# Moving GpSimd's arithmetic to VectorE in a retention layer followed by two feed-forward layers

## The chip, the cores and the metric

The kernel runs on one core of a Trainium2 chip. The metric is the device time of one execution in microseconds, as the median of several runs. The engines are TensorE (PE in the profile; its weight loads are PEld), VectorE (DVE), ScalarE (ACT), GpSimd (POOL) and SyncE (SP), which issues most DMAs.

## What is computed

The input is q, k and v of a linear attention with decay (retention), of 2 batches, 8 heads, 768 positions and head size 64, and the weights of two feed-forward layers in float64.

```python
for t in range(S):
    state = gamma * state + einsum('bhd,bhe->bhde', k[:, :, t], v[:, :, t])
    y[:, :, t] = scale * einsum('bhd,bhde->bhe', q[:, :, t], state)
x = y.transpose(0, 2, 1, 3).reshape(1536, 512)
h = x @ w_in;   x = softplus(h) @ w_out              # first layer, 512 -> 2048 -> 512
h = x @ w2_in;  y = (h * clip(h + 3, 0, 6) / 6) @ w2_out   # second layer, the same sizes
```

## The kernel before

**Attention.** The 768 positions of each batch are cut into 6 chunks of 128; a batch and a chunk make a unit, 12 in all (u = 0 to 11). A unit transposes k and q on TensorE (`transposed`, line 194), multiplies q with k and masks the result on VectorE into the tile pt (`scores`, 208), multiplies the state of the chunks before, the tile bd, with q (`carry`, 220), lets the state fade by gamma (`fade`, 261), multiplies pt with the scaled v, the tile vs (`intra`, 230; vs is made in `decayed`, 202), and adds this chunk's k times vs to the state (`state`, 244). The result is scaled into the tile on (240) and split into two tiles that TensorE takes at its fast float32 form: x_hi, a rounded copy made by ScalarE (241), and x_lo, what the copy lost (242).

**Feed-forward layers.** The 1536 rows are three chunks of 512 columns, and the 2048 inner features are 16 groups of 128. A step is one group of one chunk: `gemm1` (332) does 12 products of 128x512 (w_hi with x_hi and x_lo, w_lo with x_hi, four times), ScalarE and VectorE make the activation g in 128x512 pieces (tiles g and e) and its parts hi and lo; `gemm2` (359) does 12 more products, for the group of two steps before. The first layer has 48 steps, the second 48.

**Weights.** They arrive as pairs of 32-bit words. `convert` (83) turns one 128x512 piece of them (tile raw) into float32: ScalarE scales the high words, VectorE clamps them (a TENSOR_SCALAR raw<-raw), shifts them (a TENSOR_SCALAR w<-raw), and two SCALAR_TENSOR_TENSOR w<-raw,w put sign and low bits in. Then w is split into w_parts: ScalarE writes the high part. For the first 8 pieces (`done[1] < 2 * EARLY`, 95) GpSimd subtracts it to get the low part (97); for the 56 others ScalarE writes minus the high part and GpSimd issues a DMA that adds w to it in memory (100). There are 64 pieces; 32 of them belong to the first layer.

**Order.** Units 0 to 3 run in program order (`InOrder` with `nc.on`). From unit 4 on, each unit is followed by one step of the first layer, the pieces of weights are fed by a fixed count (`first`, 141: 6 pieces after step 0 and two more after each further step), and the order on each engine is set by the framework's scheduler. An engine works through its list in order: an instruction that waits holds all behind it. Every helper call is recorded at line 31, so the profile has to be read by tiles.

Of the kernel before, what the change touches and what calls it, by code (L numbers as in the profile page):

```python
# [10 lines left out]
F32 = mybir.dt.float32  # L11
# [3 lines left out]
ALU = mybir.AluOpType  # L15
# [26 lines left out]
def kernel(ctx, tc, q, k, v, w1_in, w1_out, w2_in, w2_out, tq, tk, tc_, tg, out):  # L42
    nc = InOrder(tc)
    B, H, S, D = q.shape
    NT, DM = out.shape
    DFF = w1_in.shape[1]
    NP = H // 2
# [35 lines left out]
    def convert(m, o, f):  # L83

        raw = raws.pop((m, o, f))
        low, y = raw[:, :, 0], raw[:, :, 1]

        w = cv_p.tile([P, CH], U32, tag="w", name="w")
        nc.scalar.activation(y.bitcast(F32), y.bitcast(F32), AF.Copy, scale=2.0 ** -112)
        nc.vector.tensor_scalar(y.bitcast(F32), y.bitcast(F32), -TOP, TOP, ALU.max, ALU.min)  # L90
        nc.vector.tensor_scalar(w, y, 3, None, ALU.logical_shift_left)
        nc.vector.scalar_tensor_tensor(w, y, 0x80000000, w, ALU.bitwise_and, ALU.bitwise_or)
        nc.vector.scalar_tensor_tensor(w, low, 29, w, ALU.logical_shift_right, ALU.bitwise_or)
        t = (wout_p if o else win_p).tile([P, 2, CH], F32R, tag="w", name="w_parts")
        if done[1] < 2 * EARLY:
            nc.scalar.activation(t[:, 0], w.bitcast(F32), AF.Copy)
            nc.gpsimd.tensor_tensor(t[:, 1], w.bitcast(F32), t[:, 0].bitcast(F32), ALU.subtract)
        else:
            nc.scalar.activation(t[:, 1], w.bitcast(F32), AF.Copy, scale=-1.0)
            nc.gpsimd.dma_start(out=t[:, 1].bitcast(F32), in_=w.bitcast(F32), accum_op=ALU.add)  # L100
            nc.scalar.activation(t[:, 0], w.bitcast(F32), AF.Copy)
        if o:
            w_out_t[m, f] = t
        else:
            w_in_t[m, f] = t.rearrange("p a (k n) -> p a k n", k=KD)
# [13 lines left out]
    def feed(n):  # L119

        n = min(n, len(order))
        while done[1] < n:
            fetch_weights(done[1] + (1 if nc.on else 2))
            convert(*order[done[1]])
            done[1] += 1
# [19 lines left out]
    s = 0  # L145
# [11 lines left out]
def attention(ctx, tc, nc, q, k, v, tq, tk, tcc, tg, x_hi, x_lo, CH, bank, feed, fetch_weights):  # L157
    B, H, S, D = q.shape
    NP = H // 2
# [18 lines left out]
    tc_sb = const.tile([P, NP], F32, name="tc_sb")  # L178
# [22 lines left out]

    def decayed(u):
        vs = wk.tile([P, H, D], F32, tag="vs" + "0" * (u < START), name="vs", bufs=2)
        (nc.vector if u < 2 else nc.gpsimd).tensor_tensor(
            vs, nat["v", u], tk_sb.rearrange("p (h o) -> p h o", o=1).to_broadcast([P, H, D]), ALU.mult)
        tr["vs", u] = vs

# [12 lines left out]
    def carry(u):  # L220
        b, i = units[u]
        qT = tr["q", u]
        o = ps(NP, C)
        tr["o", u] = o
        if i > 0:
            for p in range(NP):
                nc.tensor.matmul(o[:, p, :], bd[b][:, p, :], qT[:, p, :], start=(p == 0), stop=False, skip_group_check=True)
        fade(u)

    def intra(u):  # L230
        b, i = units[u]
        vs, pt, o = tr["vs", u], tr["pt", u], tr["o", u]
        for h in range(H):
            g = h % 2
            nc.tensor.matmul(o[g * D:(g + 1) * D, h // 2, :], vs[:, h, :], pt[:, g, h // 2, :],
                             start=(i == 0 and h < 2), stop=True, skip_group_check=True)
        c, at = divmod(u * C, CH)
        hi, lo = x_hi[c][:, :, at:at + C], x_lo[c][:, :, at:at + C]
        on = wk.tile([P, NP, C], F32, tag="on" + "0" * (u < START), name="on", bufs=2)
        nc.vector.tensor_tensor(on, o, tq_sb, ALU.mult)  # L240
        nc.scalar.activation(hi, on, AF.Copy)
        nc.gpsimd.tensor_tensor(lo, on, hi.bitcast(F32), ALU.subtract)

    def state(u):
        b, i = units[u]
# [15 lines left out]
    def fade(u):  # L261
        b, i = units[u]
        if i == 0 or i == NCH - 1:
            return
        for j in range(2):
            r = slice(j * D, (j + 1) * D)
            s = bd[b][r, :, r]
            nc.gpsimd.tensor_tensor(s, s, tc_sb[r].rearrange("p (n o) -> p n o", o=1).to_broadcast([D, NP, D]), ALU.mult)

    for t in bd:  # L270
        nc.vector.memset(t, 0.0)
# [15 lines left out]
    def prepare(u):  # L287
        transposed(u, "k")
        transposed(u, "q")
        decayed(u)  # L290
# [9 lines left out]
    for u in range(START):  # L300
        scores(u)
        prepare(u + 1)
        carry(u)
        intra(u)
        state(u)
# [5 lines left out]
    def unit(u):  # L311
        scores(u)
        if u + 3 < len(units):
            fetch(u + 3, "k", "q", "v")
        if u + 1 < len(units):
            prepare(u + 1)
        carry(u)
        intra(u)
        state(u)
# [133 lines left out]
```

## Time and profile before

| | |
|---|---|
| median of 3 runs | 620.3 us (618.93, 620.3, 621.04) |
| the profiled execution's own time | 619.72 us |
| its span on the core | 617.9 us |
| TensorE busy | 595.0 us (96%) |
| VectorE busy | 353.6 us (57%) |
| ScalarE busy | 277.5 us (45%) |
| GpSimd busy | 102.2 us (17%), 48.9 us of it in issuing 56 DMAs |
| bytes moved by DMA | 61.60 MB |

The shares are means over stages that differ: the attention units take up the first 125 us, the conversion of the first layer's weights goes on to about 170 us, and the second layer's weights are converted between about 280 and 400 us. TensorE's columns in a stretch count a product from start to its modelled end, so neighbouring products overlap.

### The profile page before, as it was taken

Reading aid. Unit: us, or ns where it says so; the run is one execution under the profiler, and the core shown is the slowest. Engines: PE = TensorE matmul, PEld = TensorE weight load, DVE = VectorE, ACT = ScalarE, POOL = GpSimd, SP = SyncE. Lnnn points to the kernel's source line nnn. Section 1 sums busy time; section 2 is a strip of 40 time slices with the busy share of each in tenths; the row PEclk is TensorE's granted clock in tenths of the full one; section 3 lists DMA queues with packets and bytes.
Section 4 is the critical chain, followed back from the end, with each engine's and each line's share of the span. In section 5 each row is a group of like instructions: output and inputs, shape, how many; then the busy total and the mean of one; then the engine's idle time right before and its main releaser. Section 6 shows DMA issues by size and latency. Waiting matters only on the chain.

```text
span 617.9 us, 7766 instructions
## 1 busy us (share of the span) xinstructions
PE 595.0 (96%) x2963; PEld 489.4 (79%) x2963; DVE 353.6 (57%) x583; ACT 277.5 (45%) x473; POOL 102.2 (17%) x110
## 2 busy tenths in 40 slices
PE   7988787999999999999999999999999999999997
PEld 6866576788888888888877878888888888888886
DVE  4599999899863433366667799822422222322223
ACT  3354556578653333465556678722222222222220
POOL 1755455432100000011111123200000000000000
PEclk9999899999999999999999999999999999999999
DMA  9998877788810000045567789700100000100001
GB/s 194 232 235 229 207 183 188 175 216 209 198 37 1 0 1 1 0 95 128 136 152 188 162 203 256 148 0 1 53 16 0 2 1 0 69 0 1 0 1 68
DMA packets 69511, 61.60 MB, mean 100 GB/s; under 512 B 40033, under 2 KB 56673, under 8 KB 69473
## 3 DMA queue, kind: packets, MB, share of 16 engines
q1 hardware_dynamic: 61408, 46.42, 26.8%
q0 software_dynamic: 8064, 14.68, 14.4%
q8 instruction: 23, 0.38, 0.3%
q14 instruction: 16, 0.12, 0.1%
HBM read 43.26 MB, written 3.15 MB: 75 GB/s over the span
## 4 chain that ended last, share of the span: by engine, by line
PE 73%; DVE 14%; DMA 5%; issue 4%; ACT 3%; SPq 1%; POOL 0%; DVEq 0%; POOLq 0%; ACTq 0%
PE banks L31 73%; DVE w L31 6%; DMA raw<-in_moe_w_in_dram 3%; DVE raw L31 2%; DVE g L31 1%; DVE pt L31 1%; DVE e L31 1%; DMA q<-in_q_dram 1%; DVE lo L31 1%; DMA w_parts<-w 1%; ACT raw L31 1%; DVE bd L31 1%; ACT e L31 1%; ACT hi L31 1%; SPq L31 1%
## 5 line engine op out<-in xcount | busy, mean ns | idle before, releaser
L31 PE MATMUL banks<-x_hi,w_parts 128*128 128x512 f32 x768 | 254.6, 392 | 0.0
L31 PEld LDWEIGHTS banks<-x_hi,w_parts 128*128 128x128 f32 x768 | 144.7, 189 | 30.9 <-issue 0.7
L31 PE MATMUL banks<-x_lo,w_parts 128*128 128x512 f32 x384 | 150.2, 391 | 0.0
L31 PE MATMUL banks<-hi,w_parts 128*128 128x512 f32 x384 | 126.9, 391 | 5.3 <-ACT w_parts L31 3.0
L31 PE MATMUL banks<-w_parts,hi 128*128 128x512 f32 (+1 forms) x386 | 118.4, 388 | 0.5 <-DVE g L31 0.5
L31 DVE SCALAR_TENSOR_TENSOR g<-e,banks 128x512 f32<-128x512 f32 x48 | 33.0, 688 | 125.2 <-ACT e L31 125.2
L31 DVE TENSOR_TENSOR lo<-g,hi 128x512 fp32r<-128x512 f32 x96 | 67.3, 701 | 48.0 <-ACT hi L31 47.9
L31 DVE SCALAR_TENSOR_TENSOR w<-raw,w 128x512 uint32<-128x512 uint32 x128 | 92.4, 723 | 1.5
L31 POOL DMA_DIRECT2D w_parts<-w x56 | 48.9, 874 | 254.3 <-ACT w_parts L31 101.0
L31 ACT ACTIVATE e<-banks,three 128x512 f32<-128x512 f32 x48 | 32.9, 685 | 127.6 <-PE banks L31 127.6
L31 PEld LDWEIGHTS banks<-hi,w_parts 128*128 128x128 f32 x384 | 71.9, 188 | 21.5 <-ACT w_parts L31 3.3
L31 ACT ACTIVATE hi<-g 128x512 fp32r<-128x512 f32 x96 | 60.5, 631 | 56.5 <-DVE g L31 56.1
L31 ACT ACTIVATE w_parts<-w 128x512 fp32r<-128x512 f32 x120 | 70.2, 624 | 34.7 <-DVE w L31 34.2
L31 PEld LDWEIGHTS banks<-w_parts,hi 128*128 128x128 f32 x386 | 72.3, 188 | 15.9 <-DVE g L31 0.9
L31 PEld LDWEIGHTS banks<-x_lo,w_parts 128*128 128x128 f32 x384 | 72.4, 189 | 15.0 <-issue 0.3
L31 PE MATMUL banks<-lo,w_parts 128*128 128x512 f32 x192 | 75.2, 392 | 0.4 <-DVE lo L31 0.4
L31 PE MATMUL banks<-w_parts,lo 128*128 128x512 f32 (+1 forms) x193 | 74.9, 388 | 0.0
L31 DVE SCALAR_TENSOR_TENSOR e<-g,banks 128x512 f32<-128x512 f32 x48 | 32.8, 684 | 32.5 <-ACT g L31 32.4
L31 ACT ACTIVATE raw<-raw 128x512 f32<-128x512 f32 x64 | 42.5, 670 | 17.1 <-DMA raw<-in_moe_w_in_dram 17.1
L31 ACT ACTIVATE g<-banks 128x512 f32<-128x512 f32 x48 | 28.4, 592 | 42.2 <-PE banks L31 42.0
L31 DVE TENSOR_TENSOR g<-g,e 128x512 f32<-128x512 f32 x48 | 33.6, 700 | 21.8 <-ACT e L31 21.2
L31 ACT ACTIVATE e<-e 128x512 f32<-128x512 f32 x48 | 30.2, 630 | 30.4 <-DVE e L31 30.1
(45 smaller groups left out, 405.7 us busy)
## 6 DMA issues: line engine op xcount, KB each, us to landing
raw<-in_moe_w_in_dram SPq DMA_DIRECT2D x32, 512.0 KB, 4.1
raw<-in_moe_w_out_dram SPq DMA_DIRECT2D x32, 512.0 KB, 4.8
w_parts<-w POOLq DMA_DIRECT2D x56, 256.0 KB, 4.5
q<-in_q_dram SPq DMA_DIRECT2D x12, 256.0 KB, 5.2
v<-in_v_dram SPq DMA_DIRECT2D x12, 256.0 KB, 5.5
k<-in_k_dram SPq DMA_DIRECT2D x11, 256.0 KB, 5.0
out_dram<-ob SPq DMA_DIRECT2D x11, 256.0 KB, 2.0
k<-in_k_dram SPq DMA_DIRECT2D x2, 128.0 KB, 2.4
```

Of the source, the lines that this page charges most:

```text
L31: ins = getattr(self.engine, op)(*args, **kwargs)
```

## The change

VectorE takes over the four kinds of arithmetic that GpSimd did: the low parts of the first 8 pieces of weights, x_lo of all 12 units, vs of units 2 to 11, and the fading of the state (two halves of 64x256 in 8 units). GpSimd keeps the 56 adding DMAs and the set-up of two constant tiles.

```diff
         if done[1] < 2 * EARLY:
             nc.scalar.activation(t[:, 0], w.bitcast(F32), AF.Copy)
-            nc.gpsimd.tensor_tensor(t[:, 1], w.bitcast(F32), t[:, 0].bitcast(F32), ALU.subtract)
+            nc.vector.tensor_tensor(t[:, 1], w.bitcast(F32), t[:, 0].bitcast(F32), ALU.subtract)
...
-        (nc.vector if u < 2 else nc.gpsimd).tensor_tensor(
+        nc.vector.tensor_tensor(
             vs, nat["v", u], tk_sb.rearrange("p (h o) -> p h o", o=1).to_broadcast([P, H, D]), ALU.mult)
...
         nc.scalar.activation(hi, on, AF.Copy)
-        nc.gpsimd.tensor_tensor(lo, on, hi.bitcast(F32), ALU.subtract)
+        nc.vector.tensor_tensor(lo, on, hi.bitcast(F32), ALU.subtract)
...
-            nc.gpsimd.tensor_tensor(s, s, tc_sb[r].rearrange("p (n o) -> p n o", o=1).to_broadcast([D, NP, D]), ALU.mult)
+            nc.vector.tensor_tensor(s, s, tc_sb[r].rearrange("p (n o) -> p n o", o=1).to_broadcast([D, NP, D]), ALU.mult)
```

The scheduler orders all engines anew. Three places of the lists follow.

VectorE in the units of fixed order, unit 1 to unit 2, before (bd_112 is the state of batch 0):

```order
L31 TENSOR_TENSOR pt<-banks,tm_sb 128x512 x2
L31 TENSOR_TENSOR on<-banks,tq_sb 128x512
L31 TENSOR_TENSOR bd_112<-bd_112,banks 64x4x64 x2
L31 TENSOR_TENSOR pt<-banks,tm_sb 128x512 x2
L31 TENSOR_TENSOR on<-banks,tq_sb 128x512
```

and with the change:

```order
L31 TENSOR_TENSOR pt<-banks,tm_sb 128x512 x2
L31 TENSOR_TENSOR vs<-v,tk_sb 128x512
L31 TENSOR_TENSOR bd_112<-bd_112,tc_sb 64x4x64 x2
L31 TENSOR_TENSOR on<-banks,tq_sb 128x512
L31 TENSOR_TENSOR x_lo_62<-on,x_hi_59 128x4x128
L31 TENSOR_TENSOR bd_112<-bd_112,banks 64x4x64 x2
L31 TENSOR_TENSOR pt<-banks,tm_sb 128x512 x2
```

Four instructions a unit have come in; x_lo stands right behind on, and the adding to the state and the next pt stand behind x_lo.

VectorE in unit 8, from its attention output on to its next pt, before (bd_113 is the state of batch 1):

```order
L31 TENSOR_TENSOR on<-banks,tq_sb 128x512 [waits PE_49,Pool_49]
L31 SCALAR_TENSOR_TENSOR w<-raw,w 128x512 [waits DVE_49]
L31 TENSOR_TENSOR bd_113<-bd_113,banks 64x4x64 [waits PE_49,Pool_49]
L31 SCALAR_TENSOR_TENSOR w<-raw,w 128x512 [waits DVE_49]
L31 TENSOR_TENSOR bd_113<-bd_113,banks 64x4x64 [waits Pool_49]
L31 TENSOR_SCALAR raw<-raw 128x512 [waits DMAHW1_49,Activation_49]
L31 TENSOR_SCALAR w<-raw 128x512 [waits DMASW0_49,DVE_49]
L31 SCALAR_TENSOR_TENSOR e<-g,banks 128x512 [waits Activation_49]
L31 SCALAR_TENSOR_TENSOR w<-raw,w 128x512 [waits DVE_49]
L31 TENSOR_SCALAR raw<-raw 128x512 [waits DMAHW4_49,Activation_49]
```

and with the change, from the pt before it on:

```order
L31 TENSOR_TENSOR pt<-banks,tm_sb 128x512 [waits PE_49] x2
L31 TENSOR_TENSOR vs<-v,tk_sb 128x512 [waits DMAHW3_49]
L31 SCALAR_TENSOR_TENSOR e<-g,banks 128x512 [waits Activation_49]
L31 TENSOR_TENSOR bd_113<-bd_113,tc_sb 64x4x64 [waits PE_49]
L31 TENSOR_TENSOR bd_113<-bd_113,tc_sb 64x4x64
L31 TENSOR_TENSOR on<-banks,tq_sb 128x512 [waits PE_49]
L31 TENSOR_TENSOR bd_113<-bd_113,banks 64x4x64 [waits DVE_49,PE_49]
L31 TENSOR_TENSOR bd_113<-bd_113,banks 64x4x64 [waits DVE_49]
L31 TENSOR_TENSOR x_lo_64<-on,x_hi_61 128x4x128 [waits Activation_49]
L31 TENSOR_TENSOR g<-g,e 128x512
L31 TENSOR_SCALAR raw<-raw 128x512 [waits DMAHW2_49]
L31 TENSOR_SCALAR raw<-raw 128x512 [waits DMAHW5_49]
```

The attention's instructions now stand together right behind pt, the pieces of weights behind them, two side by side, and the waits for GpSimd are gone.

TensorE at the last unit, from its carry on, before:

```order
L31 MATMUL banks<-qT,bd_113 128x128 x3
L31 MATMUL banks<-x_hi_59,w_parts 128x512 [waits DVE_49]
L31 MATMUL banks<-x_lo_62,w_parts 128x512
L31 MATMUL banks<-x_hi_59,w_parts 128x512 [waits DMASW3_49]
L31 MATMUL banks<-x_hi_59,w_parts 128x512
L31 MATMUL banks<-pt,vs 64x128 [waits DVE_49,Pool_49]
```

and with the change:

```order
L31 MATMUL banks<-qT,bd_113 128x128 x3
L31 MATMUL banks<-x_hi_59,w_parts 128x512
L31 MATMUL banks<-x_lo_62,w_parts 128x512
L31 MATMUL banks<-x_hi_59,w_parts 128x512 [waits DMASW3_49]
L31 MATMUL banks<-x_hi_59,w_parts 128x512
L31 MATMUL banks<-x_lo_62,w_parts 128x512
L31 MATMUL banks<-x_hi_59,w_parts 128x512 x2
L31 MATMUL banks<-x_lo_62,w_parts 128x512
L31 MATMUL banks<-x_hi_59,w_parts 128x512 x2
L31 MATMUL banks<-x_lo_62,w_parts 128x512
L31 MATMUL banks<-x_hi_59,w_parts 128x512
L31 MATMUL banks<-pt,vs 64x128 [waits DVE_49]
```

TensorE's list has 12 products of step 7 instead of 4 ahead of the first product that needs the last unit's pt.

## Rows read from the trace of the kernel before

**Rows 1.** Busy time of each engine by stretch; PEclk, DMA share, GB/s stand last.

```profile
28.00:121.00 93.00, 78.33 (x549) 62.04 (x550) 87.99 (x137) 53.22 (x95) 49.93 (x44) 0.96 0.83 205
121.00:165.00 44.00, 44.00 (x204) 36.06 (x204) 40.53 (x76) 33.46 (x60) 11.94 (x13) 1.00 0.87 210
```

**Rows 2.** Chain that ended last, after 150 us: start, length, what.

```profile
149.94 132.39 PE banks L31 x584
...
361.91 251.94 PE banks L31 x1113
```

**Rows 3.** Waits of PE between 28 and 127 us: total, times, longest.

```profile
PE banks L31 <- DVE pt L31: 8.7, 8, 2.7
PE banks L31 <- ACT w_parts L31: 3.0, 1, 3.0
PE banks L31 <- POOL w_parts L31: 2.2, 2, 1.5
```

**Rows 4.** Groups of VectorE, 28 to 121 us: count, busy us, mean ns, idle before.

```profile
L31 DVE SCALAR_TENSOR_TENSOR w<-raw,w 128x512 uint32<-128x512 uint32 x39 | 30.2, 777 | 0.2
L31 DVE TENSOR_SCALAR raw<-raw 128x512 f32<-128x512 f32 x20 | 15.0, 751 | 0.1
L31 DVE TENSOR_SCALAR w<-raw 128x512 uint32<-128x512 uint32 x20 | 13.6, 682 | 0.2
...
L31 DVE TENSOR_TENSOR lo<-g,hi 128x512 fp32r<-128x512 f32 x7 | 5.9, 838 | 0.0
```

**Rows 5.** The same groups, 121 to 165 us.

```profile
L31 DVE TENSOR_SCALAR raw<-raw 128x512 f32<-128x512 f32 x14 | 5.8, 423 | 1.5 <-ACT raw L31 1.5
...
L31 DVE TENSOR_TENSOR lo<-g,hi 128x512 fp32r<-128x512 f32 x7 | 4.8, 685 | 0.0
```

**Rows 6.** Timeline around 46 us, VectorE and GpSimd: start, length, what.

```profile
46.69 1.49 DVE L31 TENSOR_SCALAR raw<-raw 128x512 f32<-128x512 f32 x1
...
46.44 1.46 POOL L31 TENSOR_TENSOR x_lo<-on,x_hi 128x512 fp32r<-128x512 f32 x1
```

**Rows 7.** Groups of GpSimd's arithmetic, 28 to 121 us.

```profile
L31 POOL TENSOR_TENSOR x_lo<-on,x_hi 128x512 fp32r<-128x512 f32 x8 | 11.8, 1472 | 0.5 <-ACT x_hi L31 0.5
L31 POOL TENSOR_TENSOR w_parts<-w,w_parts 128x512 fp32r<-128x512 f32 x8 | 11.4, 1429 | 17.3 <-ACT w_parts L31 17.3
...
L31 POOL TENSOR_TENSOR bd<-bd,tc_sb 64x256 f32<-64x256 f32 x10 | 9.5, 952 | 7.8 <-PE banks L31 7.5
L31 POOL TENSOR_TENSOR vs<-v,tk_sb 128x512 f32<-128x512 f32 x7 | 8.3, 1181 | 1.1 <-DMA v<-in_v_dram 0.9
```

**Rows 8.** Timeline of VectorE: four instructions between unit 3 and unit 11.

```profile
26.92 0.69 DVE L31 TENSOR_TENSOR on<-banks,tq_sb 128x512 f32<-128x512 f32 x1 [1.72 <-issue]
...
89.27 0.69 DVE L31 SCALAR_TENSOR_TENSOR e<-g,banks 128x512 f32<-128x512 f32 x1
...
97.23 0.41 DVE L31 TENSOR_TENSOR bd<-bd,banks 64x256 f32<-64x256 f32 x1
...
120.05 1.28 DVE L31 TENSOR_TENSOR pt<-banks,tm_sb 128x512 f32<-128x512 f32 x2
```

**Rows 9.** One stretch behind a wait of TensorE, columns as in rows 1.

```profile
66.00:70.00 4.00, 3.86 (x12) 3.19 (x13) 4.00 (x6) 2.87 (x5) 1.69 (x2) 0.58 1.10 325
```

**Rows 10.** Timelines of PE (two scores) and ACT (x_hi) in units 2 and 3.

```profile
17.60 1.16 PE L31 MATMUL banks<-qT,kT 64*128 64x128 f32 x16
...
22.72 1.16 PE L31 MATMUL banks<-qT,kT 64*128 64x128 f32 x16
...
22.53 0.63 ACT L31 ACTIVATE x_hi<-on 128x512 fp32r<-128x512 f32 x1 [2.00 <-DVE on L31]
```

**Rows 11.** Piece 27 (w_out 11): its adding DMA, gemm2 using it; page: landing.

```profile
146.31 0.89 POOL L31 DMA_DIRECT2D w_parts<-w  x1 [2.18 <-ACT w_parts L31]
...
157.03 0.39 PE L31 MATMUL banks<-hi,w_parts 128*128 128x512 f32 x1
...
w_parts<-w POOLq DMA_DIRECT2D x56, 256.0 KB, 4.5
```

## The prediction

> **What bounds the kernel now.** I read the stretches first [rows 1]. Between 28 and 121 us, where attention units and steps alternate, VectorE is busy 87.99 of 93.00 us and TensorE 78.33; from 121 to 165 us TensorE is busy without a gap. The chain that ended last says the same of the rest: it lies on TensorE's products for 132 us up to 282 and for 252 us from 362 us to the end [rows 2]. So the time is set in two ways: TensorE works off a fixed list after about 121 us, and what comes before is as late as VectorE makes it. A microsecond gained before 121 us is gained at the end, if the weights keep up; the stretch between 282 and 362 us starts when TensorE releases the first layer's weights, so it moves along.
>
> Then I looked at what TensorE waits for up to 127 us: 8.7 us for pt in 8 waits, 3.0 and 2.2 us for w_parts [rows 3], all results of VectorE or, through w, of VectorE and GpSimd. The reader should see that these are waits for a place in VectorE's list, not for its speed on one tile.
>
> The decisive view is VectorE's groups, compared over two stretches. Between 28 and 121 us the TENSOR_SCALAR that clamps takes 751 ns, the shift 682, the SCALAR_TENSOR_TENSOR 777 and lo 838 [rows 4]; between 121 and 165 us, where GpSimd hardly computes, the clamp takes 423 and lo 685 [rows 5]. The timeline shows why: the clamp at 46.69 took 1.49 us and ended at 48.18, as GpSimd's x_lo, begun at 46.44, ended at 47.90 [rows 6]. It stood still until GpSimd was through. The sum of these **blocks** between 28 and 121 us is 20 x (751 - 423) = 6.6, 20 x (682 - 423) = 5.2 (the shift priced like the clamp), 39 x (777 - 685) = 3.6 (the SCALAR_TENSOR_TENSOR priced like lo, of the same size) and 7 x (838 - 685) = 1.1, together **16.5 us**.
>
> **The change, part by part.**
>
> *Removed.* GpSimd's 33 instructions of that stretch, 41.0 us of its time [rows 7]; with them the 16.5 us of blocks.
>
> *Added on VectorE.* In the same stretch 8 x_lo, 8 low parts, 7 vs of 128x512, and 10 halves of the fading. What one costs I take from a stretch without blocks: from the e at 89.27 to the bd at 97.23 [rows 8] VectorE starts 11 instructions of the 0.69 kind and 4 of the 0.41 kind in 7.96 us, which is 11 x 0.60 + 4 x 0.34. So 23 x 0.60 + 10 x 0.34 = **17.2 us**. The fading on VectorE (two inputs in SBUF, 64x256) is not in the trace; its bounds are 0.34 (the start distance of a short one) and 0.60 (that of a 128x512 one, twice as long), and I take 0.34, as the adding to bd of the same shape took 0.41 from start to end [rows 8]. The upper end would add 2.6 us.
>
> A rule speaks against this price. By the Trainium skill (VectorE: DVE Perf Modes, "The DRAIN you can't avoid") the next VectorE instruction does not start until the one before has left the pipeline. By it the 23 would cost their full 0.69 and the 10 their 0.41, 20.0 us, and the forecast below would be 2.8 us higher. The rows disagree: starts lie 0.60 apart where one lasts 0.69.
>
> Arithmetic added and blocks removed thus nearly cancel, 17.2 against 16.5. What decides is VectorE's **standing still** and the new order of its list.
>
> *The sum.* I measure VectorE from on of unit 3 to the last unit's second pt: 26.92 to 121.33 before [rows 8], 94.4 us. Its list there holds 84 long instructions (8 on, 16 pt, 39 SCALAR_TENSOR_TENSOR, 7 each of e, g, lo) and 54 short ones (20 clamps, 20 shifts, 14 on bd): 84 x 0.60 + 54 x 0.34 = 68.8. With 16.5 of blocks, 9.1 us are left as standing still (5.0 of it idle in rows 1) and as hand-overs between instructions that need each other's result.
>
> The new list holds 104 long ones (7 vs, 8 x_lo and 8 low parts more, but 36 SCALAR_TENSOR_TENSOR) and 60 short ones (10 fadings more, but 18 clamps and 18 shifts): two pieces of weights have slipped behind the last pt. That is 104 x 0.60 + 60 x 0.34 = 82.8 us, without blocks.
>
> *The start.* In units 1 to 3 TensorE needs 5.12 us per unit [rows 10]. VectorE's loop becomes two pt 1.20, vs 0.60, two fadings 0.68, on 0.69, the wait for ScalarE's x_hi 0.63 [rows 10], x_lo 0.60, two additions 0.68: 5.1 us. So it just holds the pace, but the first time x_lo holds up the addition to the state and pt; walking through the list I come to on of unit 3 about **1.0 us** later than before. GpSimd did this beside them.
>
> *The end of the attention.* TensorE's new list has 8 more products ahead of the last pt than the old one, worth 8 x 0.226 = **1.8 us** (0.226 is 251.94/1113, rows 2).
>
> *Standing still in the new list.* With the same 9.1 us the gain is 94.4 - 1.0 - 82.8 - 9.1 + 1.8 = 3.3; with none it is 12.4. I take 6: between the ends, nearer the upper one for standing still, since x_hi, carry and intra are still waited for; less than now, because the raw pieces stand in pairs, so that a shift no longer waits for the clamp just ahead of it, and because pt reaches TensorE sooner. **Gain 94.4 - 1.0 - 82.8 - 6.0 + 1.8 = 6.4 us.**
>
> *The clock.* Behind a long wait TensorE ran with a granted clock of 0.58 in the mean of 66 to 70 us [rows 9], at half speed for most of it; such a stretch costs 4 x 0.42 = 1.7 us, and there is one more like it before 121 us. I count no gain from them: where VectorE sets the pace they are hidden, and the new list has a long wait ahead of unit 6's pt (6 pieces of weights and 5 low parts stand before it).
>
> *Do the weights keep up?* The last piece with little room is number 27: its adding DMA was issued at 146.31, lands about 4.5 us later at 150.8, and the third product of gemm2 at 157.03, at 157.5, needs it [rows 11]: 6.7 us of room. Up to there VectorE's sum is changed by 17.2 - 16.5 and by the 1.0 of the start, and less standing still (9.1 - 6) gives 3.1 back, so it lands about 1.4 earlier. TensorE can be 6.7 + 1.4 = 8.1 us earlier before it waits for weights. 6.4 fits, hardly more: this is the next thing to be late.
>
> *At no cost:* GpSimd issues its DMAs sooner and waits for less; they are not held back now either (0.89 us for the one at 146.31, with VectorE busy).
>
> The profiled execution took 619.7 us, 0.6 below the median of the runs; 619.7 - 6.4 = 613.3, and on the median's scale 613.9. I forecast **613.6 us**.
>
> **The rivals.**
>
> *No difference.* VectorE does as much as before, so nothing moves. That is so if standing still grows from 9.1 to between 10.5 and 14.3 us, when the gain is within 1.9 us (0.3%, about what a measurement of this kernel can tell from no change): about **620 us**. For it: the sums nearly cancel, and VectorE now also waits for v's DMAs and for carry. Against it: two pieces slipped behind and the 1.8 us ahead of the last pt don't depend on standing still.
>
> *Slower: the closed loop.* GpSimd's instructions waited for carry and x_hi without holding anyone; on VectorE's list these waits hold all behind them. If nothing fills them, each of the 8 units from 4 on waits for carry and intra, 12 of 32 products of 5.12 us, thus 1.9, less vs and two fadings in between, 0.6 left, and 0.63 for x_hi: 8 x 1.23 = 9.8 us above the 9.1. The gain of 3.3 becomes a loss of 6.5: **626 us**. It decides from 0.65 us added per unit (3.3 + 1.9 over 8). For it: units 0 to 2 have x_lo right behind on. Against it: in unit 8's list e stands ahead of the fading and the two additions ahead of x_lo.
>
> *More than forecast.* Standing still disappears and the half clock with it: 12.4 us, cut by the weights to about 11: **609 us**. Against it: attention still passes from VectorE to TensorE and back in each unit.
>
> **How the numbers follow.** Forecast and more-than-forecast, 0.80 together (0.62 and 0.18); no difference 0.12; slower 0.08. The ends of the gain, 3.3 and 12.4, are 617 and 607.3 us on the median's and the execution's own scale; with the dear fading (2.6) the upper one comes to 619. The range 607 to 619 leaves out the slower case, the upper part of no difference, and a little below.
>
> **What would show it.** Right: the clamp and the shift near 423 ns and lo near 685 everywhere; no TensorE wait for GpSimd; VectorE's last pt ending near 117 us; x_lo on VectorE at 0.69, a fading at about 0.41; units 8 to 11 at 10 to 11 us each; TensorE without gaps from there to the second layer's weights. Wrong: VectorE's last pt at 121 us or later with unblocked instructions, idle time behind x_hi or carry in each unit (the loop), TensorE waits for w_parts after 120 us (the weights), or instructions on VectorE that stay long without GpSimd's arithmetic beside them (then the blocks had another cause, and the sum falls).

## The result and the profile after

The changed kernel took 623.23 us (median of 7 runs, 621.83 to 623.79), the kernel before 620.25 us beside it (7 runs, 618.93 to 621.18). The ratio is 1.0055, with a 95% interval of 1.0044 to 1.0065: **slower by half a percent**, where 613.6 us and a gain were forecast. The profiled execution has a span of 621.4 us, against 617.9.

The change did what it was to do on VectorE. These are its groups between 28 and 121 us in the changed kernel (count, busy us, mean ns, idle before); they answer to [rows 4]:

```profile
L31 DVE SCALAR_TENSOR_TENSOR w<-raw,w 128x512 uint32<-128x512 uint32 x36 | 24.1, 684 | 0.0
...
L31 DVE TENSOR_SCALAR w<-raw 128x512 uint32<-128x512 uint32 x19 | 7.9, 422 | 0.0
L31 DVE TENSOR_SCALAR raw<-raw 128x512 f32<-128x512 f32 x19 | 7.5, 423 | 0.0
...
L31 DVE TENSOR_TENSOR x_lo<-on,x_hi 128x512 fp32r<-128x512 f32 x8 | 5.5, 689 | 0.2
L31 DVE TENSOR_TENSOR w_parts<-w,w_parts 128x512 fp32r<-128x512 f32 x8 | 5.5, 687 | 1.0 <-ACT w_parts L31 1.0
...
L31 DVE TENSOR_TENSOR bd<-bd,tc_sb 64x256 f32<-64x256 f32 x12 | 5.0, 417 | 0.2
```

The clamp is back at 423 ns (751 before), the shift at 422 (682), the SCALAR_TENSOR_TENSOR at 684 (777): the blocks are gone. So the question is where that time went. The stretches of [rows 1], in the changed kernel:

```profile
28.00:121.00 93.00, 86.45 (x594) 67.73 (x591) 88.33 (x170) 53.27 (x93) 8.87 (x10) 0.96 0.78 189
121.00:165.00 44.00, 38.89 (x169) 31.24 (x168) 39.62 (x75) 33.10 (x58) 10.39 (x12) 0.98 0.90 212
```

Up to 121 us TensorE got more done (594 records against 549). Between 121 and 165 us it is busy 38.89 of 44.00 us, where it had no gap before. The gaps, in TensorE's timeline (start, length, what, and in brackets the idle time before it with its releaser):

```profile
142.46 0.73 PE L31 MATMUL banks<-hi,w_parts 128*128 128x512 f32 x2 [0.25 <-DMA w_parts<-w]
...
149.42 0.74 PE L31 MATMUL banks<-hi,w_parts 128*128 128x512 f32 x2 [1.23 <-DMA w_parts<-w]
...
164.68 1.65 PE L31 MATMUL banks<-hi,w_parts 128*128 128x512 f32 x3 [3.63 <-DMA w_parts<-w]
```

All three are waits for an adding DMA, 5.11 us together; the kernel before has none there. Behind the last one the granted clock stands at the lower of its two levels (1.2 of 2.4 GHz), as the stretches show:

```profile
160.00:165.00 5.00, 1.37 (x6) 0.87 (x5) 3.53 (x7) 2.73 (x5) 0.86 (x1) 0.83 0.92 192
165.00:170.00 5.00, 5.00 (x13) 3.84 (x13) 0.84 (x2) 1.50 (x3) 0.00 (x0) 0.50 0.36 105
170.00:175.00 5.00, 5.00 (x23) 4.15 (x22) 4.00 (x8) 3.47 (x7) 1.75 (x2) 0.99 0.66 153
```

From 165 to 170 us TensorE ran 13 products at 0.50, where 170 to 175 us has 23 at 0.99: 5 x 0.5 = 2.5 us lost. From there on the chain is as before, only later:

```profile
157.80 6.84 DMA w_parts<-w
164.68 121.62 PE banks L31 x524
...
365.30 251.98 PE banks L31 x1113
```

The balance: the first gemm1 that follows the attention (step 8) begins 4.57 us earlier, and gemm2 of step 13 begins 3.97 us later. TensorE's timeline in the kernel before, and then in the changed kernel:

```profile
127.11 0.39 PE L31 MATMUL banks<-x_hi,w_parts 128*128 128x512 f32 x1
...
167.91 0.39 PE L31 MATMUL banks<-hi,w_parts 128*128 128x512 f32 x1
```

```profile
122.54 0.39 PE L31 MATMUL banks<-x_hi,w_parts 128*128 128x512 f32 x1
...
171.88 0.39 PE L31 MATMUL banks<-hi,w_parts 128*128 128x512 f32 x1
```

So 8.54 us were lost between the two. The three waits are 5.11 of them, and 0.16 us more each, because products otherwise start 0.23 us apart while one lasts 0.39. The half clock takes 2.7 (20 products in the 7.20 us from 164.68 to 171.88, which take 4.5 at full clock). The last 0.3 us is not followed. Of the 3.97 us, 0.6 comes back where the second layer's weights are converted: the last part of the chain starts 3.39 us later than before (365.30 against 361.91, [rows 2]), and the span grew by 3.5.

The piece behind the longest wait is number 29 (w_out of group 12), which gemm2 of step 12 needs after its first products. Three engines hand over its lateness. VectorE, ScalarE and GpSimd in the changed kernel:

```profile
153.26 0.69 DVE L31 SCALAR_TENSOR_TENSOR w<-raw,w 128x512 uint32<-128x512 uint32 x1
155.43 0.69 DVE L31 SCALAR_TENSOR_TENSOR e<-g,banks 128x512 f32<-128x512 f32 x1 [1.48 <-ACT g L31]
156.04 0.69 DVE L31 SCALAR_TENSOR_TENSOR w<-raw,w 128x512 uint32<-128x512 uint32 x1
```

```profile
154.80 0.60 ACT L31 ACTIVATE g<-banks 128x512 f32<-128x512 f32 x1 [1.67 <-PE banks L31]
...
156.76 1.15 ACT L31 ACTIVATE w_parts<-w 128x512 fp32r<-128x512 f32 x2
```

```profile
157.80 0.86 POOL L31 DMA_DIRECT2D w_parts<-w  x1 [3.91 <-ACT w_parts L31]
```

The first SCALAR_TENSOR_TENSOR of the piece is done at 153.95. The second stands behind e, e waits for ScalarE's g, and g for TensorE's gemm1, which had itself been held up by the wait of 1.23 us at 149.42. So one wait for weights makes the next piece of weights late. Then its DMA landed 6.84 us after its issue, while two raw transfers of 512 KB, issued at 156.75 and 157.13, were under way.

### The profile page after: what moved, and what is told of

Same layout as the page of the kernel before. It is cut to its first block, busy times and chain, and to the rows that moved or that the text cites. A ratio compares the mean times of both kernels' runs of the same rounds, so it can differ in the third digit from the quotient of the medians.

```text
span 621.4 us, 7689 instructions
## 1 busy us (share of the span) xinstructions
PE 601.8 (97%) x2963; PEld 493.0 (79%) x2963; DVE 359.2 (58%) x629; ACT 278.5 (45%) x473; POOL 49.9 (8%) x64
## 4 chain that ended last, share of the span: by engine, by line
PE 70%; issue 10%; DVE 7%; DMA 6%; ACT 3%; POOL 2%; SPq 1%; POOLq 0%; DVEq 0%; ACTq 0%
PE banks L31 70%; DMA raw<-in_moe_w_in_dram 3%; DVE w L31 3%; DMA w_parts<-w 2%; POOL w_parts L31 2%; DVE raw L31 1%; SPq L31 1%; DVE g L31 1%; DVE lo L31 1%; DMA v<-in_v_dram 1%; ACT raw L31 1%; ACT e L31 1%; ACT hi L31 1%; ACT w_parts L31 1%; DVE e L31 1%
## 5 line engine op out<-in xcount | busy, mean ns | idle before, releaser
L31 PE MATMUL banks<-hi,w_parts 128*128 128x512 f32 x384 | 130.7, 400 | 9.7 <-DMA w_parts<-w 5.1
L31 DVE SCALAR_TENSOR_TENSOR w<-raw,w 128x512 uint32<-128x512 uint32 x128 | 87.5, 687 | 1.4
L31 PEld LDWEIGHTS banks<-lo,w_parts 128*128 128x128 f32 x192 | 36.8, 192 | 8.3 <-DVE lo L31 0.8
```

What stands on the lines that cost most here:

```text
L31: ins = getattr(self.engine, op)(*args, **kwargs)
```

## The experiments

**Theory A**: the first layer's last pieces come late because VectorE's list is full up to 160 us, and two pieces have slipped behind the attention. **Theory B**: piece 29 alone is late, because its adding DMA meets the raw transfers, of the second layer above all. **Theory C**: the loss lies ahead of 121 us. All kernels below are the changed one with an edit, unless said otherwise.

**e1**, to move the second layer's transfers:

```diff
-            fetch_weights(done[1] + (1 if nc.on else 2))
+            fetch_weights(min(done[1] + (1 if nc.on else 2), 2 * NF if done[1] < 2 * NF else 4 * NF))
```

> The changed kernel, but the second layer's raw weights are not fetched before the first layer's 32 pieces are converted; the order of VectorE, ScalarE and TensorE is that of the changed kernel. Theory A (VectorE's list between 121 and 160 us is full, and the first layer's last pieces are ready late whatever the DMAs do): the adding DMA of piece 29 lands in about 4.5 instead of 6.84 us, so TensorE's longest wait for w_parts falls only from 3.63 to about 1.3 us; time 621 to 622.5. Theory B (the adding DMA of piece 29 is late because it shares the DMA engines with the second layer's raw transfers): that wait and the half clock behind it (some 2.5 us) go; time 617 to 618.5. If the transfers have no part in it: 623, as the changed kernel.

622.91 us, ratio 1.0054 (1.0041 to 1.0066). The experiment missed its aim: the scheduler put the fetch where it had been (156.45 us instead of 157.13), the landing stayed at 6.5 us and the wait at 3.31. It says nothing on the theories.

**e2**, two pieces more ahead:

```diff
-                feed(first(f))
+                feed(first(f) + 2)
```

> The changed kernel, fed two pieces of weights more after each step, so that about 20 instead of 18 pieces are converted ahead of the last attention unit, as in the kernel before. Theory A (the two pieces that slipped behind the attention are what comes late at 142 to 168 us): TensorE's three waits for adding DMAs after 121 us (0.25, 1.23, 3.63 us) and the half clock behind the last go, about 7.6 us; in return two pieces, 2 x 1.9 us of VectorE, stand ahead of the last pt, so that it ends about 123 instead of 119.2 us; the sum is 3 to 4 us better than the changed kernel: 619 to 620.5. Theory B (only the meeting with the second layer's transfers costs): the same meeting occurs earlier or not at all, the waits stay in part; 621 to 624. Theory C (the loss lies in the attention part): slower than the changed kernel by the 3.8 us, 625 to 627.

616.07 us, ratio 0.9944 (0.9930 to 0.9958): **faster than both kernels**. Behind 121 us TensorE has no wait and full clock:

```profile
121.00:165.00 44.00, 44.00 (x203) 36.04 (x203) 40.14 (x76) 34.43 (x62) 11.47 (x14) 1.00 0.92 223
```

The last pt ends at 121.58 instead of 119.2 us, and gemm1 of step 8 begins at 123.51, only 0.97 later than in the changed kernel. Piece 29's DMA is issued at 153.18, 4.6 us earlier than in the changed kernel. That is theory A's mechanism, at a lower price than I gave the two pieces: the time lies below all three of the expectations. C falls.

**e3**, the low parts of pieces 2 to 7 by adding DMAs (`done[1] < 2` in line 95):

> The changed kernel, but VectorE makes the low part of the first 2 pieces alone; those of pieces 2 to 7 come from adding DMAs like the other 56. That takes 6 x 0.60 = 3.6 us off VectorE between 28 and 60 us, and lays 6 waits of 4.5 us for a DMA in the place of 6 subtractions. Theory A (VectorE's sum of work up to 160 us sets both the last pt and the last pieces): everything behind comes 3.6 us earlier, last pt at 115.6, the waits after 121 us stay as they are since both move alike; 619.5 to 620.5. Rival (TensorE's wait of 3.97 us at 58 us, for a w_parts, is as long or longer with a DMA in the chain, and it is this that sets the pace): no gain or a loss, 623 to 626.

622.36 us, ratio 1.0053 (1.0032 to 1.0073), the same as the changed kernel: no gain, as the rival said. TensorE waits 6.9 us for adding DMAs between 28 and 127 us, and 4.7 us behind 121. Work taken off VectorE came back as four waits for transfers.

**e4**, x_lo on GpSimd again (line 242):

> The changed kernel with x_lo alone given back to GpSimd, all 12 of them. The first units lose the wait for x_hi: unit 3's on about 1.9 us earlier, at 26.9 us. From unit 4 on VectorE has 8 x 0.60 = 4.8 us less of its own and 8 x 0.59 = 4.7 us of standing still beside GpSimd's instructions more (its share, 11.8 of 41.0 us, of the 16.5 us of before). Theory A: a gain of the 1.9 us of the start alone, 621 to 622. Rival (x_lo on VectorE also holds up its list by the wait for x_hi in the later units): 8 x 0.5 more, 617 to 618. Rival (what counts is that VectorE stands still beside GpSimd): no change or slower, 623 to 625.

619.22 us, ratio 0.9991 (0.9974 to 1.0007), between two of the expectations. Its attention is *later* than in the changed kernel (gemm1 of step 8 at 125.49 against 122.54), and yet it ends earlier: there is no wait behind 121 us, since TensorE comes later and piece 29's DMA earlier (154.69). An attention that is 2.95 us slower gave a kernel that is 0.6% faster.

**e5**, the second layer's first raw tile tied to piece 32 (beside the edit of e1):

```diff
+        if (m, o, f) == (1, 0, 0):
+            nc.scalar.activation(raw[:, 0:1, 0].bitcast(F32), w_out_t[0, NF - 1][:, 0, 0:1].bitcast(F32), AF.Copy)
```

> The changed kernel, with the second layer's first raw weights made to wait for the 32nd piece of the first layer (a one-column ScalarE copy of that piece into the raw tile ahead of its fetch); the run before this, which only moved the fetch in the program, left the transfers at 156.45 us. Theory B (piece 29's adding DMA is late because of the second layer's transfers): it lands in 4.5 instead of 6.84 us, TensorE's wait of 3.63 us falls to 1.3 us or goes, and with it the half clock (2.5 us): 618 to 619.5 on the scale of 623 for the changed kernel, ratio to before 0.997 to 0.999. Theory A (the pieces are ready late on VectorE and ScalarE, 4.8 us after one another there, whatever the DMAs do): a wait of 1.3 us or more stays, and the waits at 142 and 149 us stay; 621 to 622.5, ratio 1.001 to 1.004. If the second layer's weights come too late by it, TensorE waits for them at about 285 us.

617.8 us, ratio 0.9976 (0.9967 to 0.9986), in theory B's range. One of the second layer's fetches still went at 155.59; the next went at 168.74, and the first layer's last raw piece had been issued by 148.2. So one raw transfer lay beside piece 29's DMA in place of two. Its landing (count, KB, us from issue) in the changed kernel, and then in e5:

```profile
w_parts<-w POOLq DMA_DIRECT2D x1, 256.0 KB, 6.8
```

```profile
w_parts<-w POOLq DMA_DIRECT2D x1, 256.0 KB, 4.9
```

It was also issued 1.17 us earlier, and so landed 3.1 us earlier; the attention, too, was 1.03 us earlier in this run (gemm1 of step 8 at 121.51), which the edit does not explain. TensorE's waits and clock in e5:

```profile
148.22 0.74 PE L31 MATMUL banks<-hi,w_parts 128*128 128x512 f32 x2 [1.25 <-DMA w_parts<-w]
154.30 0.73 PE L31 MATMUL banks<-hi,w_parts 128*128 128x512 f32 x2 [0.31 <-DMA w_parts<-w]
161.54 0.97 PE L31 MATMUL banks<-hi,w_parts 128*128 128x512 f32 x3 [1.05 <-DMA w_parts<-w]
```

```profile
165.00:170.00 5.00, 5.00 (x24) 4.14 (x23) 3.14 (x6) 3.22 (x7) 1.75 (x2) 1.00 0.46 76
```

The waits are 2.61 instead of 5.11 us, and the clock stayed up. Theory A's waits stayed in part (1.25 us at 148.22, 1.05 us for piece 29); e2 removes them as well. How much of e5's gain belongs to the transfers is not shown cleanly: of the 3.1 us by which piece 29 landed earlier, 2.0 are the shorter landing and 1.17 the earlier issue.

**e6**, the kernel *before* with e2's edit:

> The kernel before (GpSimd computes), fed two pieces more after each step. It tells whether the changed kernel with two pieces ahead, which took 0.9944 of before, gains by the change or by the feed alone. If by the feed alone: 0.993 to 0.996 here too. If by the change (VectorE has nothing to gain in the kernel before, where no wait for adding DMAs stands behind 121 us, and the two pieces only put the last pt 3 to 4 us later): 1.004 to 1.008, about 622 to 625 us.

618.42 us, ratio 0.9987 (0.9975 to 0.9998): neither. The feed alone brings 0.13%, so most of e2's 0.56% is the move of the arithmetic, which pays once the weights keep up.

**e7**, e2 and e4 together:

> The changed kernel with two pieces more ahead and x_lo given back to GpSimd. Each alone took about 1% and 0.6% off the changed kernel. If they take off different things (the feed the waits behind 121 us, x_lo the 1.9 us of the start): 0.991 to 0.993 of before. If the same thing (each only brings the pieces of weights in time behind 121 us): 0.996 to 0.999, no better than x_lo on GpSimd alone, since GpSimd's instructions make VectorE stand still again and no wait is left to take away.

616.65 us, ratio 0.9959 (0.9947 to 0.9971), at the edge of the second case: both take away the same waits.

**e8**, four pieces ahead (`first(f) + 4`):

> The changed kernel, fed four pieces more after each step; 22 pieces stand ahead of the last pt. If two were enough to end TensorE's waits behind 121 us, the two further ones only put the last pt later, by 2 x 1.9 us, from 121.6 to about 125: 0.999 to 1.001 of before. If attention and steps still have slack for them: 0.993 to 0.995, as with two.

624.58 us, ratio 1.0084 (1.0071 to 1.0097), slower than expected. The last pt ends at 126.4, 4.8 us later than in e2, where 3.8 were expected for two pieces more. The rest I had not thought of: a wait where the second layer's weights begin to be converted, with the lower clock behind it.

```profile
285.31 0.79 PE L31 MATMUL banks<-hi,w_parts 128*128 128x512 f32 x1 [2.40 <-ACT hi L31]
```

```profile
288.00:292.00 4.00, 4.00 (x11) 3.17 (x10) 1.78 (x4) 3.03 (x6) 0.00 (x0) 0.50 0.65 162
```

ScalarE's hi waits for VectorE's g, and on VectorE's list a shift of the next piece of weights stands ahead of g and waits for an adding DMA, issued at 276.05, that lands 7.4 us later:

```profile
283.50 0.43 DVE L31 TENSOR_SCALAR w<-raw 128x512 uint32<-128x512 uint32 x1 [5.10 <-DMA w_parts<-w]
283.85 0.68 DVE L31 TENSOR_TENSOR g<-g,e 128x512 f32<-128x512 f32 x1
```

```profile
284.62 0.63 ACT L31 ACTIVATE hi<-g 128x512 fp32r<-128x512 f32 x1 [5.89 <-DVE g L31]
```

This time the weights hold up the steps, on the same list.

**e9**, x_lo of units 0 to 3 alone on GpSimd:

```diff
-        nc.vector.tensor_tensor(lo, on, hi.bitcast(F32), ALU.subtract)
+        (nc.gpsimd if u < START else nc.vector).tensor_tensor(lo, on, hi.bitcast(F32), ALU.subtract)
```

> The changed kernel with x_lo of units 0 to 3 alone given back to GpSimd; behind unit 3 the lists stay nearly as they are. It prices the start by itself. The on of unit 3 comes at 26.9 instead of 28.79 us. If the start is a term of VectorE's whole list (the pieces of weights come 1.9 us earlier with the attention, the waits behind 121 us stay the same length): 621.1 on the scale of 623, ratio to before 1.002 to 1.004. If it is a term of the attention alone, and the weights come when they do: no gain, 1.005 to 1.007.

616.59 us, ratio 0.9963 (0.9950 to 0.9977), several times the expected gain. The on of unit 3 comes at 26.96, as expected, and gemm1 of step 8 at 120.68. Piece 29's DMA is issued 1.22 us earlier than in the changed kernel and lands in 4.8 us; the longest wait behind 121 us is 1.33 and the clock stays at 1.00 there. One raw transfer was issued just ahead of that DMA (155.53) where the changed kernel has two. So 1.8 us at the start also took the kernel out of the meeting of transfers and out of the half clock.

**e10**, e2 and e9 together:

> Both together: two pieces more ahead, and x_lo of units 0 to 3 on GpSimd. With the waits behind 121 us gone (the changed kernel with two pieces ahead took 0.9944 of before), the 1.9 us of the start should come on top: 0.991 to 0.992, 613.5 to 614.5 us. If the start is swallowed by a wait further on (the 3.1 us for w_parts at 61 us): 0.994 to 0.995.

614.2 us, ratio 0.9916 (0.9902 to 0.9929), as expected and the fastest of all: 0.84% under the kernel before.

**e11** and **e12**, e2 with the low parts of the first 8 pieces, or with vs and the fading, back on GpSimd:

> The changed kernel with two pieces ahead, the low parts of the first 8 pieces given back to GpSimd. By the sums of the prediction it makes no difference: 8 x 0.60 = 4.8 us less of VectorE's own work, 11.4 of 41.0 us of the 16.5 us of standing still more, 4.6 us: 0.993 to 0.996. If TensorE's wait for a w_parts at 58 to 61 us (3.1 us, half clock behind it) comes from the low parts in VectorE's list: it falls to 1.5 us or less, 0.988 to 0.991. If GpSimd's 1.43 us in place of 0.69 lengthens that wait: 0.997 to 1.0.

> The changed kernel with two pieces ahead, vs of units 2 to 11 and the fading given back to GpSimd; low parts and x_lo stay on VectorE. By the sums: 7 x 0.60 + 10 x 0.34 = 7.6 us less on VectorE, 17.8 of 41.0 us of the 16.5 us of standing still more, 7.2 us: 0.993 to 0.996. If the fading and vs on VectorE hold up its list by their waits for carry and for v: faster, 0.989 to 0.992. If what counts is the standing still beside GpSimd's instructions: slower, 0.997 to 1.0, as the kernel before with two pieces ahead (0.9987).

616.51 us, ratio 0.9958 (0.9945 to 0.9970), and 617.22 us, 0.9967 (0.9956 to 0.9978); e2 has 0.9944. In e11 the sums hold: from on of unit 3 to the end of piece 29 VectorE takes 123.6 us, and 123.4 in e2. Behind 121 us it has one wait for weights, 0.93 us for piece 29. e12 lies between its first and its third case, and the sums do not settle it: VectorE gets through the same stretch in 118.6 us, but gemm1 of step 8 begins at 124.33, 0.8 us later than in e2; why was not followed. That vs and the fading are better off on VectorE by 0.2% is on the edge of what the intervals tell.

**What the runs have in common.** Behind gemm2 of step 12 TensorE's list takes about the same time, 453.3 to 456.7 us. In us, with the first product of that gemm2 that takes piece 29's low part:

| | gemm1 of step 8 | piece 29's DMA issued | landed | first product with it | span | span less product | span less gemm1 of step 8 |
|---|---|---|---|---|---|---|---|
| before | 127.11 | 152.94 | 159.1 | 162.92 | 617.9 | 455.0 | 490.8 |
| after | 122.54 | 157.80 | 164.6 | 164.68 | 621.4 | 456.7 | 498.9 |
| e2 | 123.51 | 153.18 | 159.2 | 159.37 | 614.5 | 455.1 | 491.0 |
| e4 | 125.49 | 154.69 | 159.0 | 161.30 | 616.8 | 455.5 | 491.3 |
| e5 | 121.51 | 156.63 | 161.5 | 161.54 | 615.7 | 454.2 | 494.2 |
| e9 | 120.68 | 156.58 | 161.4 | 161.41 | 614.7 | 453.3 | 494.0 |
| e10 | 121.99 | 151.66 | 156.2 | 157.85 | 612.4 | 454.6 | 490.4 |

(After: 2.5 of the 456.7 are the half clock. In after, e5 and e9 two or three more products stand ahead of this one.) Where TensorE waits for no weights behind step 8 (before, e2, e4, e10), the span is 490.4 to 491.3 us longer than the start of gemm1 of step 8: there a microsecond of the attention is one at the end, as the prediction said. Where it waits, the difference is 494.0 to 498.9 us. So e9, with the earliest attention, is behind e10, which has no wait.

What the change did shows in the first two rows. In the kernels without a wait (before, e2, e4, e10) the product comes 35.8 to 35.9 us behind gemm1 of step 8. In the changed kernel it was thus due 4.57 us earlier than before, while its DMA was issued 4.86 us later and took 0.65 us longer to land: 10.1 us, against 3.8 us of room. The meeting of transfers is not new: piece 29 meets raw transfers in the kernel before and in e2 too, and lands in 6.2 and 6.0 us, in time. So A says what went wrong, and two pieces more ahead (e2) take all the waits away. In e5 and e9 a shorter landing and an earlier issue together take away a part of the waits and the half clock; B's share by itself stays open. C falls (e4, e9).

## Why the prediction was wrong

*Blocks.* Right: 423, 422 and 684 ns, as forecast. The moved instructions took 0.69 and 0.42 us.

*The fading and the start.* Mis-sized. VectorE's timeline of unit 2 in the changed kernel:

```profile
23.20 0.69 DVE L31 TENSOR_TENSOR on<-banks,tq_sb 128x512 f32<-128x512 f32 x1
24.59 0.69 DVE L31 TENSOR_TENSOR x_lo<-on,x_hi 128x512 fp32r<-128x512 f32 x1 [0.70 <-ACT x_hi L31]
25.20 0.86 DVE L31 TENSOR_TENSOR bd<-bd,banks 64x256 f32<-64x256 f32 x2
26.09 1.29 DVE L31 TENSOR_TENSOR pt<-banks,tm_sb 128x512 f32<-128x512 f32 x2
27.29 0.68 DVE L31 TENSOR_TENSOR vs<-v,tk_sb 128x512 f32<-128x512 f32 x1
27.89 0.86 DVE L31 TENSOR_TENSOR bd<-bd,tc_sb 64x256 f32<-64x256 f32 x2
28.79 0.69 DVE L31 TENSOR_TENSOR on<-banks,tq_sb 128x512 f32<-128x512 f32 x1
```

Two halves on bd take 0.89 or 0.90 us from start to the next instruction, not 2 x 0.34 = 0.68. So the loop is 5.59 us (23.20 to 28.79) and not 5.1, and does not hold TensorE's pace of 5.12. The on of unit 3 came 1.87 us later (28.79 against [rows 8]), not 1.0. With 0.44 instead of 0.34 the ten fadings cost 1.0 us more; the upper end of 2.6 held. The trace of the kernel before shows the price: its pair of additions to bd in unit 3 takes 0.90 us to the next start. I had gone by the length of a single one (97.23, [rows 8]).

```profile
28.05 0.87 DVE L31 TENSOR_TENSOR bd<-bd,banks 64x256 f32<-64x256 f32 x2 [0.43 <-PE banks L31]
28.95 0.43 DVE L31 TENSOR_SCALAR raw<-raw 128x512 f32<-128x512 f32 x1
```

The two halves lie in partitions 0 to 63 and 64 to 127; the second starts 0.44 after the first, whose length is 0.42, while 128x512 instructions start 0.60 apart at a length of 0.69 (27.29 to 27.89). By the Trainium skill (VectorE: DVE Perf Modes, "Two Vector instructions with no wait between them") an instruction whose operands start in another group of 32 partitions than those of the instructions before it starts only when these have finished. The trace agrees with that, 0.44 against 0.42. So of the two kinds that the prediction priced, the halves start as the rule on the DRAIN has it, and the 128x512 instructions do not.

*The attention.* The direction was right: 4.57 us earlier at gemm1 of step 8, where 6.4 was forecast; 0.9 of the difference is the start and 1.0 the fading. The last pt ended at 119.2, not near 117. Up to it the sum held: VectorE took 90.4 us from on of unit 3, which is the 82.8 of its list, 1.0 for the fading and 6.6 of standing still, where 6.0 was taken.

*"Do the weights keep up?"* **This is the step that failed**, in three places.
- It took piece 27 for the last with little room. Piece 29 had less: in the kernel before its DMA was issued at 152.94 and landed 6.2 us later, at 159.1, for a product at 162.92. The room was 3.8 us and not 6.7, less than the gain I forecast. The trace of before shows this; I had looked at one piece with the median landing of 4.5 us. Issue, first product and landing in the kernel before:

```profile
152.94 0.86 POOL L31 DMA_DIRECT2D w_parts<-w  x1 [1.72 <-ACT w_parts L31]
...
162.92 0.62 PE L31 MATMUL banks<-hi,w_parts 128*128 128x512 f32 x2
...
w_parts<-w POOLq DMA_DIRECT2D x1, 256.0 KB, 6.2
```

- It let the weights land 1.4 us earlier. They came later: the DMA of piece 27 by 3.67 us (149.98 against [rows 11]), that of piece 29 by 4.86. From on of unit 3 to the end of piece 29 VectorE works off 28 long and 9 short instructions more than before (counted in both timelines), 28 x 0.60 + 9 x 0.34 = 19.9 us, for 16.5 us of blocks: 3.4 us, and 1.87 from the start, less 0.4 of standing still. Of the 28, 24 are the moved ones; the other 4 are e, g and lo of steps that TensorE now reached earlier. An earlier TensorE takes VectorE's time from the very pieces that it will need. So of the 3.1 us of standing still that I gave back only 0.4 came back up to there: it is 127.94 - 116.08 = 11.86 us (the stretch less the list of 147 long and 82 short), against 124.96 - 96.22 - 16.5 = 12.24 (119 long and 73 short).
- It gave a wait the price of its length. The wait of 3.63 us cost 2.5 us more in clock.

*The rivals.* The closed loop, the slower case of the forecast, did not come in the form given: x_hi is waited for 0.70 us in each of units 0 to 2 and hardly later (0.2 us idle in all before the 8 x_lo of 28 to 121 us). The loop that closed runs over the weights, VectorE to TensorE and back. What would show it was named: waits of TensorE for w_parts after 120 us.

## What to carry to other kernels

Where an engine serves two streams, here the attention and the conversion of weights, the sum of its work says little on the end: ask which of the streams the scheduler will put first, and measure the room of the other at every piece that is near its use, with that piece's own landing. A gain that only one stream makes is a loan; feeding two pieces earlier (e2) turned +0.55% into -0.56%. And a hand-over that is free on an idle engine, such as x_lo behind x_hi in units of fixed order, is better left there (e9, e10).

## What was not expected of the hardware

Behind waits of TensorE of 3.63 us (the changed kernel), 2.40 (e8) and 2.14 with one of 1.52 close behind it (e11, at 63.14 and 65.63) the granted clock was 0.50 in the stretches of 165 to 170, 288 to 292 and 66 to 68 us. After waits of 1.05 to 1.33 us (e5, e9, and the changed kernel at 149.42), after one of 2.02 (e6, at 94.48) and even after one of 3.29 (e3, at 53.86), it stayed at 1.00. So the length of the one wait does not tell which it will be. The wait of 3.63 us cost 2.5 us more in this way.

The adding DMA of piece 29, always 256 KB, landed in 5.8 to 6.9 us in the six kernels with two raw transfers of 512 KB issued 0.6 to 1.1 us ahead of it (the changed kernel, e1, e2, e3, e11, e12). With a single one issued 1.0 us ahead it landed in 4.2 to 4.9 us (the seven kernels e4 to e10); the kernel before, where an earlier one was still under way beside that one, has 6.2.
